# A fused attention, cosine layer and expert layer: the second token tile is summed in two parts, and four attention halves use another product form

## The chip, the cores and the metric

The kernel runs on one core of one Trainium2 chip. The metric is the device time of one execution in microseconds (us). Below, PE is the matrix engine (TensorE), DVE the vector engine (VectorE), ACT the scalar engine (ScalarE), POOL is GpSimd, and SP is the engine whose queue issues nearly all DMAs here. Every engine works through its own queue in order, and waits on semaphores for the others.

## The reference

Three steps follow each other, all in fp32.

```python
scores = scale * q @ k.T                      # 4 batches x 8 heads, 768 positions, 64 wide
keep   = (pos < n_sink) | (0 <= i - j < window)   # 4 first keys, and a window of 128
x  = softmax(where(keep, scores, -1e9)) @ v   # -> 3072 tokens x 512
h  = x @ w_in                                 # 512 -> 2048
y  = (h * cos(h)) @ w_out                     # 2048 -> 512
e  = argmax(y @ w_gate + bias[modality])      # one of 8 experts for each token
out = gate * relu(y @ w1[e]) @ w2[e]
```

The weights `w_in` and `w_out` come as 64-bit floats, and the kernel turns them into fp32 itself.

## The kernel before

Each fp32 product is made of three faster ones: an operand is split into a high part (`_h`, `_l` for the rest), and high by high, high by low and low by high are summed in PSUM. ACT copies the high part out of PSUM, DVE or POOL subtracts it to get the low part.

**Halves and tiles.** The 3072 tokens are 8 tiles of 384 (`NTILE`, numbers 0 to 7). Tile n is half a batch: even n the first 384 positions (three key blocks of 128), odd n the last 384 (four key blocks). The attention of one tile is called a half; it goes over 4 pairs of heads (`attn_front`, `mid`, `rest`). In `rest`, the normalised scores `Pb` are turned by PE (`pt`), split into `pT_h` and `pT_l`, the 16 columns of the first keys are copied out into `pc` and turned as well (`pz`, then `sp`), and the product with `v` is summed in `po`. From `STACK` on, a half uses the "stacked" form of the scores: both parts of a head lie over each other on 128 rows. The halves before it use 64 rows for each head, so two heads' products run beside each other.

**Blocks.** The cosine layer works on one tile and one slice `f` of 128 of the 2048 columns at a time; that is a block, 16 to a tile (`ffn_tile_gen`). A block makes `hp` (12 products of 384 columns on PE), DVE and ACT make `ch`, and ACT and POOL split it into `g_h` and `g_l`. Two blocks later its 9 products of 512 columns go into the three sums `y`. While the blocks of tile n - 1 run, the attention of tile n is woven in between: `run_ffn` emits as many blocks as a table of weights (`ATT_STEPS`, `STEPS_0`, `STEPS_1`) says. The list `seq` gives the order of blocks: 6 blocks of tile 0 (`F0`), 16 each of tiles 1 to 7, and the other 10 of tile 0 at the end. Between, the three partial sums of tile 0 lie in DRAM (`yp_scr`) and so do its inputs (`xs_scr`).

**Conversion.** `conv_gen` turns one slice of `w_in` and one of `w_out` for each of the 16 values of `f`: five DVE operations `cv_a` and one ACT operation for each of the 32 pieces, and the low part on POOL. `conv_to` paces it: 8 steps ahead, 4 steps a block in tile 0, and the rest over 16 blocks (`CSP`) of tile 1. A scheduler may move an instruction against its neighbours within the dependences.

**Routing.** When a tile's sum is complete, `route_tile` turns it (`yT`, 12 transposes), multiplies by the gate weights (`pl`, 12 products), picks the expert and stores the row. For the expert layer, tokens of one expert are gathered 256 at a time (a page, T = 0 to 13): `gather` computes the row numbers on DVE and issues two indirect DMAs on POOL into `m_yg`, `prelude` turns them (`m_a`), `first_product` and `second_product` follow, and the result is scattered to `out`. A page with 128 tokens or fewer takes the short form (`first_product_half`, `turn_half`). When the expert changes, `split` makes the new weights' high part on ACT and their low part on DVE for even and on POOL for odd pieces; `run(T)` gathers page T + 1 at its start.

Of the kernel before, what the change touches and what calls it, by code (L numbers as in the profile page):

```python
# [20 lines left out]
P = 128  # L21
# [15 lines left out]
STACK = 3  # L37
# [24 lines left out]
def kernel(  # L62
# [45 lines left out]
    xs_scr = [dram.tile([P, NPAIR * HALF], F32, name=f"xs_scr{i}") for i in range(2)]  # L108
    yp_scr = dram.tile([NQ, P, DM], F32, name="yp_scr")
# [129 lines left out]
    vp = apool.tile([P, 4, 5 * D], F32R, name="vp")  # L239
# [163 lines left out]
    def attn_front(hb, pr):  # L403
# [37 lines left out]
        kT_h = apool.tile([P, 4, SEG], F32R, name="kT_h")  # L441
# [6 lines left out]
        kT_l = kl[0]  # L448
# [20 lines left out]
        bs = [P, nblk - 1, NS]  # L469
        bj = [D, nblk - 1, NS]  # L470
        if stack:
            for j in range(2):
# [3 lines left out]
                if half == 0:  # L476
                    DVE.tensor_copy(ks_h[r, pr, :], kT[j][r, 0, 0:NS].bitcast(F32))
                    DVE.tensor_copy(ks_l[r, pr, :], kl[j][r, 0, 0:NS].bitcast(F32))
                DVE.tensor_copy(kT[j][r, 0:nblk - 1, P:SEG], ks_h[r, pr:pr + 1, :].to_broadcast(bj))
                DVE.tensor_copy(kl[j][r, 0:nblk - 1, P:SEG], ks_l[r, pr:pr + 1, :].to_broadcast(bj))  # L480
                kf = kT[j].rearrange("p t s -> p (t s)")[:, 0:nblk * SEG - NS].bitcast(F32)
                SP.dma_start(out=kf[hr[1 - j]], in_=kf[r])
        else:
            ACT.activation(out=kT_h[:, 0:nblk, 0:P], in_=pk3[:, 0:nblk, :], func=AF.Copy)
            tt(DVE, kT_l[:, 0:nblk, 0:P], pk3[:, 0:nblk, :], kT_h[:, 0:nblk, 0:P].bitcast(F32), ALU.subtract)
            if half == 0:
                DVE.tensor_copy(ks_h[:, pr, :], kT_h[:, 0, 0:NS].bitcast(F32))
                DVE.tensor_copy(ks_l[:, pr, :], kT_l[:, 0, 0:NS].bitcast(F32))
            DVE.tensor_copy(kT_h[:, 0:nblk - 1, P:SEG], ks_h[:, pr:pr + 1, :].to_broadcast(bs))
            DVE.tensor_copy(kT_l[:, 0:nblk - 1, P:SEG], ks_l[:, pr:pr + 1, :].to_broadcast(bs))  # L490
# [66 lines left out]
        def rest():  # L557
# [45 lines left out]
            xs = apool.tile([P, HALF], F32, name="xs")  # L603
# [9 lines left out]
            for j in range(2):  # L613
# [11 lines left out]
            ACT.activation(out=xh[:, pr, :], in_=xs, func=AF.Copy)  # L625
            tt(POOL, xl[:, pr, :], xs, xh[:, pr, :].bitcast(F32), ALU.subtract)
# [32 lines left out]
    def span(i):  # L659
        return (F0 if i == NTILE else 0), (F0 if i == 0 else NF)  # L660

    def start_of(i):
        return seq.index((i, span(i)[0]))

    def ffn_tile_gen(ypool_of):
        LAG = 2
# [23 lines left out]
        for c in range(n_all + LAG):  # L690
# [28 lines left out]
            if c == n_all + LAG - 3:  # L719
# [4 lines left out]
                ysb[NTILE] = [ypool_of().tile([P, YC], F32, name="yt", bufs=NQ) for _ in range(NQ)]  # L724
                for t in range(NQ):
                    SP.dma_start(out=ysb[NTILE][t][:, 0:DM], in_=yp_scr[t])
            i, f = seq[c - LAG] if c >= LAG else (0, -1)
            if f == span(i)[1] - 1:
                if i == 0:

                    for t in range(NQ):
                        yt = mpool.tile([P, DM], F32, name="y_part", tag="wo_l", bufs=WL_BUFS)
                        ACT.activation(out=yt, in_=yps[0][t], func=AF.Copy)
                        SP.dma_start(out=yp_scr[t], in_=yt)
                elif i == NTILE:
# [3 lines left out]
                    ysb[0] = ysb.pop(NTILE)  # L739
# [636 lines left out]
```

## Time and profile before

| what | value |
|---|---|
| median of three runs | 1231.5 us (1226.4 to 1232.37) |
| profiled execution | 1229.5 us, its span 1227.7 us |
| PE, DVE, ACT, POOL busy | 93%, 66%, 58%, 32% of the span |
| granted PE clock, mean | 0.963 of 2.4 GHz |

A busy PE is not a PE at its peak: a product counts as busy from its start to its modelled end, and products overlap. So the stretches with a slow clock and with gaps tell more than the mean. The stretch from 0 to 45 us is the first half's attention alone; blocks 0 to 5 run up to about 145 us, the 16 of tile 1 up to about 275 us, the 16 of tile 2 up to about 375 us, and the expert layer starts near 886 us.

### The profile page before, as it was taken

Reading aid. Unit: us, or ns where it says so; the run is one execution under the profiler, and the core shown is the slowest. Engines: PE = TensorE matmul, PEld = TensorE weight load, DVE = VectorE, ACT = ScalarE, POOL = GpSimd, SP = SyncE. Lnnn points to the kernel's source line nnn. Section 1 sums busy time; section 2 is a strip of 40 time slices with the busy share of each in tenths; the row PEclk is TensorE's granted clock in tenths of the full one; section 3 lists DMA queues with packets and bytes.
Section 4 is the critical chain, followed back from the end, with each engine's and each line's share of the span. In section 5 each row is a group of like instructions: output and inputs, shape, how many; then the busy total and the mean of one; then the engine's idle time right before and its main releaser. Section 6 shows DMA issues by size and latency. Waiting matters only on the chain. (4 is left out here: it accounts for less than half of the span.)

```text
span 1227.7 us, 21801 instructions
## 1 busy us (share of the span) xinstructions
PE 1143.7 (93%) x6560; PEld 1004.5 (82%) x6560; DVE 814.1 (66%) x2357; ACT 711.7 (58%) x1479; POOL 396.2 (32%) x422
## 2 busy tenths in 40 slices
PE   4878879889999999999999999999999999799995
PEld 3667767778988888988889888989889988699994
DVE  7788889987787788788878877464762224621220
ACT  4677667678876788777678876333422224522221
POOL 3655536552222322322232222142311113611110
PEclk9778888899999999999999999999999999899998
DMA  6444345533342333334324422361324113311210
GB/s 149 130 151 120 90 130 179 159 103 93 89 100 70 78 99 104 80 79 106 80 68 117 96 69 94 93 234 54 101 98 153 37 45 105 113 37 47 61 37 24
DMA packets 141338, 118.86 MB, mean 97 GB/s; under 512 B 98415, under 2 KB 107631, under 8 KB 141168
## 3 DMA queue, kind: packets, MB, share of 16 engines
q1 hardware_dynamic: 136848, 103.29, 30.5%
q0 software_dynamic: 4320, 13.65, 3.5%
q8 instruction: 65, 1.06, 0.4%
q14 instruction: 105, 0.86, 0.2%
HBM read 151.32 MB, written 19.67 MB: 139 GB/s over the span
## 5 line engine op out<-in xcount | busy, mean ns | idle before, releaser
L148 POOL TENSOR_TENSOR g_l<-ch,g_h 128x384 fp32r<-128x384 f32 x128 | 131.8, 1031 | 410.1 <-ACT g_h L715 393.7
L136 PE MATMUL hp<-xT_h,wi_h 128*128 128x384 f32 x512 | 184.7, 362 | 5.8 <-DVE ch L148 5.7
L136 PE MATMUL hp<-xT_h,wi_l 128*128 128x384 f32 x512 | 177.8, 347 | 0.0
L136 PE MATMUL hp<-xT_l,wi_h 128*128 128x384 f32 x512 | 177.6, 347 | 0.0
L643 PE MATMUL y<-wo,g_h 128*128 128x512 f32 x384 | 160.1, 417 | 0.0
L643 PE MATMUL y<-wo_l,g_h 128*128 128x512 f32 x384 | 157.9, 411 | 0.0
L643 PE MATMUL y<-wo,g_l 128*128 128x512 f32 x384 | 155.5, 405 | 0.2 <-POOL g_l L148 0.2
L136 PE MATMUL m_y<-wi_h,hT 128*128 128x512 f32 x416 | 134.1, 397 | 0.6 <-issue 0.4
L145 DVE SCALAR_TENSOR_TENSOR hT<-m_h,hT 128x256 fp32r<-128x256 f32 x88 | 37.3, 424 | 142.3 <-ACTq L1292 93.5
L705 ACT ACTIVATE ch<-ch,half_pi 128x384 f32<-128x384 f32 x128 | 78.8, 616 | 79.7 <-DVE ch L145 78.5
L136 PEld LDWEIGHTS hp<-xT_h,wi_h 128*128 128x128 f32 x512 | 99.3, 194 | 12.2 <-DVE ch L148 6.7
L136 PEld LDWEIGHTS hp<-xT_l,wi_h 128*128 128x128 f32 x512 | 99.3, 194 | 4.8 <-issue 0.7
L136 PEld LDWEIGHTS hp<-xT_h,wi_l 128*128 128x128 f32 x512 | 99.2, 194 | 0.7 <-issue 0.2
L142 DVE TENSOR_SCALAR ch<-hp 128x384 int32<-128x384 f32 x128 | 71.1, 555 | 41.8 <-PE hp L136 27.7
L715 ACT ACTIVATE g_h<-ch 128x384 fp32r<-128x384 f32 x128 | 66.5, 519 | 49.1 <-DVE ch L148 38.0
L136 PEld LDWEIGHTS m_y<-wi_h,hT 128*128 128x128 f32 x416 | 79.1, 190 | 17.1 <-issue 0.8
L1143 POOL DMA_INDIRECT out_dram<-m_ot,m_ids x26 | 26.3, 1011 | 204.9 <-ACT m_ot L1142 183.3
L554 ACT ACTIVATE Pb<-Pb,mx 128x272 f32<-128x272 f32 (+1 forms) x168 | 82.7, 493 | 11.5 <-DVE mx L538 10.4
L148 DVE TENSOR_TENSOR ch<-ch,hp 128x384 f32<-128x384 f32 x128 | 70.3, 550 | 24.8 <-ACT ch L705 23.2
L1111 ACT ACTIVATE hT<-m_h 128x256 fp32r<-128x256 f32 x88 | 33.7, 383 | 90.1 <-PE m_h L136 86.8
L643 PEld LDWEIGHTS y<-wo,g_l 128*128 128x128 f32 x384 | 73.2, 191 | 14.0 <-POOL g_l L148 0.7
L136 PE MATMUL m_y<-wi_l,hT 128*128 128x512 f32 x208 | 81.8, 393 | 0.0
(297 smaller groups left out, 3032.0 us busy)
## 6 DMA issues: line engine op xcount, KB each, us to landing
rw<-in_moe_w_dram SPq DMA_DIRECT2D x112, 512.0 KB
wo_l<-wl_scr SPq DMA_DIRECT2D x122, 256.0 KB
cv_in<-in_moe_w_in_dram SPq DMA_DIRECT2D x16, 512.0 KB
cv_out<-in_moe_w_out_dram SPq DMA_DIRECT2D x16, 512.0 KB
y_scr<-yt SPq DMA_DIRECT2D x24, 256.5 KB
xT_h<-xg_h SPq DMA_DIRECT2D x32, 192.0 KB
xT_l<-xg_l SPq DMA_DIRECT2D x32, 192.0 KB
qn<-in_q_dram SPq DMA_DIRECT2D x56, 96.0 KB
```

Source lines behind the costliest of these rows:

```text
L136: PE.matmul(o, l, r, start=start, stop=stop)
L142: e.tensor_scalar(out=o, in0=i, scalar1=s1, scalar2=s2, op0=op0, op1=op1)
L145: e.scalar_tensor_tensor(out=o, in0=i0, scalar=s, in1=i1, op0=op0, op1=op1)
L148: e.tensor_tensor(out=o, in0=a, in1=b, op=op)
L554: ACT.activation(out=Pb[t][j][:, c0:c1], in_=Pb[t][j][:, c0:c1], func=AF.Exp, scale=-1.0, bias=mx[:, i:i + 1], accum_out=sm[:, i:i + 1])
L643: i = PE.matmul(o, l, r, start=start, stop=stop)
L705: ACT.activation(out=ch, in_=ch, func=AF.Sin, scale=TWO_PI, bias=half_pi)
L715: ACT.activation(out=gh, in_=ch, func=AF.Copy)
L1111: ACT.activation(out=hT_h[f], in_=hp, func=AF.Relu)
L1143: POOL.indirect_dma_start(out=out[:, :], out_offset=bass.IndirectOffsetOnAxis(ap=m_ids[T % 4][:, h:h + 1], axis=0), in_=m_ot[h], in_offset ...
```

## The change

- **Order of blocks.** Tile 1 is summed in two parts as tile 0 is: its first 12 blocks (`F1`) stand where they stood, its last 4 come after tile 7 and ahead of tile 0's last 10. Its partial sums and inputs go through DRAM as well, and its routing comes at the end. Rows of `y_scr` are stored in the order of tiles 2 to 7, 1, 0.
- **Conversion.** `conv_to` spreads the steps after tile 0 over 12 blocks of tile 1 and 12 blocks of tile 2.
- **Halves 0 to 3** (`STACK` is 4) take another form of the product with `v`: both heads are summed in one `po`, with zeros beside each head's columns in `vp`. That is three products for each head and key block and not two, one copy on ACT and one subtraction on DVE for each pair; the two `xs` copies and two additions, and POOL's subtraction, are gone. Half 3 was stacked before and is not now.
- **POOL.** In halves 0 to 3 (`NPOOL` is 4) `pc` is copied on POOL and not on DVE; half 3's scaling of `Pb` goes to POOL too.
- **Small merges.** `ks_h` and `ks_l` become one tile, so two copies and two casts become one each.
- **Expert layer.** `split` uses DVE alone. The row numbers of page T + 2 are computed in page T, and its gather is issued ahead of page T's last scatter. The lead expert's weights are split in blocks near the end, some five later than before against the list.

```diff
-STACK = 3
+STACK = 4
-PB2 = 3
+PB2 = 4
+F1 = 12
-NPOOL = 3
+NPOOL = 4
-seq = [(i, f) for i in range(NTILE) for f in range(F0 if i == 0 else NF)] + [(NTILE, f) for f in range(F0, NF)]
+cut = {0: F0, 1: F1}
+late_of = {NTILE: 1, NTILE + 1: 0}
+seq = [(i, f) for i in range(NTILE + 2) for f in range(*span(i))]
...
-                        DVE.tensor_copy(pc[:, t, j], Pb[t][j][:, P:SEG])
+                        POOL.tensor_copy(pc[:, t, j], Pb[t][j][:, P:SEG])
...
+            if not stack:
+                po = psb("po")
+                mm(po[:, 0:HALF], vs[:, 0:2 * D], sp, True, False)
+                mm(po[:, 0:HALF], vs[:, 2 * D:4 * D], sp, False, False)
+                for j in range(2):
+                    for blk in range(nblk):
+                        c0, c1, m0, m1 = band(blk)
+                        vh, vl = [vp[:, blk, (o + j) * D:(o + j + 2) * D] for o in (0, 3)]
+                        mm(po[:, c0:c1], vh, pT_h[:, j, m0:m1], False, False)
+                        mm(po[:, c0:c1], vh, pT_l[:, j, m0:m1], False, False)
+                        mm(po[:, c0:c1], vl, pT_h[:, j, m0:m1], False, j == 1 and blk == nblk - 1)
+                ACT.activation(out=xh[:, pr, :], in_=po[:, 0:HALF], func=AF.Copy)
+                tt(DVE, xl[:, pr, :], po[:, 0:HALF], xh[:, pr, :].bitcast(F32), ALU.subtract)
...
-        tt(DVE if f % 2 == 0 else POOL, dst_l, src, dst_h.bitcast(F32), ALU.subtract)
+        tt(DVE, dst_l, src, dst_h.bitcast(F32), ALU.subtract)
...
-            with maybe(cond):
-                gather(T + 1, flags[T + 1, "col"])
+            with maybe(cond2):
+                gather_rows(T + 2, val(3, T + 2, (ET.DVE,), NV - 1))
+            def after():
+                with maybe(cond2):
+                    gather_go(T + 2)
...
-            second_product(T, 1, m_y[1])
+            second_product(T, 1, m_y[1], None, after)
```

Three places show how instructions moved.

PE, the product with `v` of one pair of heads in the third half, before: one head's products (the other head's seven follow, into another `po`).

```order
L136 MATMUL po<-sp,vs 128x384
L136 MATMUL po<-pT_h,vp 128x256
L136 MATMUL po<-pT_l,vp 128x256
L136 MATMUL po<-pT_h,vp 128x256
L136 MATMUL po<-pT_l,vp 128x256
L136 MATMUL po<-pT_h,vp 128x128
L136 MATMUL po<-pT_l,vp 128x128
```

The same place now: one head's part, after the two `sp` products that serve both heads.

```order
L137 MATMUL po<-sp,vs 128x384 x2
L137 MATMUL po<-pT_h,vp 128x256
L137 MATMUL po<-pT_l,vp 128x256
L137 MATMUL po<-pT_h,vp 128x256 x2
L137 MATMUL po<-pT_l,vp 128x256
L137 MATMUL po<-pT_h,vp 128x256
L137 MATMUL po<-pT_h,vp 128x128
L137 MATMUL po<-pT_l,vp 128x128
L137 MATMUL po<-pT_h,vp 128x128
```

Each key block has a third product, so a pair has 20 products and not 14 (26 and not 18 where there are four key blocks).

POOL, one pair of the third half beside tile 1, before (`wi_l`, `wo_l` are low parts of the conversion, `g_l` of a block).

```order
L142 TENSOR_SCALAR Pb<-Pb,sm 128x128 x2
L142 TENSOR_SCALAR Pb<-Pb,sm 128x272 x4
L148 TENSOR_TENSOR wi_l_2119<-cv_a,wi_h_2113 128x512
L148 TENSOR_TENSOR g_l<-ch,g_h 128x384
L148 TENSOR_TENSOR wo_l<-cv_a,wo_123 128x512
```

And now.

```order
L149 TENSOR_TENSOR wo_l<-cv_a,wo_121 128x512
L143 TENSOR_SCALAR Pb<-Pb,sm 128x128 x2
L143 TENSOR_SCALAR Pb<-Pb,sm 128x272 x2
L149 TENSOR_TENSOR g_l<-ch,g_h 128x384
L143 TENSOR_SCALAR Pb<-Pb,sm 128x272 x2
L601 COPY pc<-Pb 128x32
```

The copy `pc` stands on POOL right behind the pair's last scaling; on DVE it is gone.

POOL, end of one page of the expert layer (the long form's end is a scatter of half 0 and of half 1), before: the next page's two gathers come behind all of it, at the start of the next `run`.

```order
L148 TENSOR_TENSOR wi_l_95<-rw_9677,wi_h_85 128x512
L1292 UNCONDITIONAL_BRANCH x2
L1143 DMA out_dram<-m_ot_9707,m_ids_9696 3072x512
L1318 ISA
L1318 UNCONDITIONAL_BRANCH
L1255 TENSOR_LOAD tab_i x2
L1088 DMA m_yg_9681<-y_scr,m_idg_9694 128x513
L1088 DMA m_yg_9682<-y_scr,m_idg_9694 128x513
```

And now, the long form.

```order
L1191 DMA out_dram<-m_ot_10086,m_ids_10075 3072x512
L1134 DMA m_yg_10056<-y_scr,m_idg_10073 128x513
L1134 DMA m_yg_10057<-y_scr,m_idg_10073 128x513
L1191 DMA out_dram<-m_ot_10087,m_ids_10075 3072x512
L1374 UNCONDITIONAL_BRANCH
```

The gathers (of the page after the next) stand between the two scatters, and no `wi_l` is left on POOL.

## Rows read from the trace of the kernel before

**Rows 1.** The page: the span, and the granted PE clock in 40 slices.

```profile
span 1227.7 us, 21801 instructions
...
PEclk9778888899999999999999999999999999899998
```

**Rows 2.** Busy time by stretch; columns as the first line says.

```profile
core 0: us, PE busy (x) PEld busy (x) DVE busy (x) ACT busy (x) POOL busy (x), PEclk, DMA share, GB/s
0.00:45.00 45.00, 27.41 (x114) 20.72 (x114) 32.93 (x138) 23.57 (x66) 19.52 (x32) 0.97 0.56 137
45.00:145.00 100.00, 83.45 (x407) 67.67 (x407) 83.70 (x229) 70.27 (x169) 57.32 (x69) 0.77 0.42 121
145.00:275.00 130.00, 111.87 (x560) 91.40 (x559) 116.83 (x256) 92.92 (x192) 70.08 (x75) 0.91 0.50 146
275.00:375.00 100.00, 97.65 (x585) 87.27 (x584) 81.51 (x248) 79.06 (x155) 26.25 (x28) 1.00 0.38 92
1049.00:1056.00 7.00, 5.78 (x18) 4.78 (x18) 4.54 (x8) 5.11 (x12) 5.71 (x5) 0.52 0.85 278
```

**Rows 3.** DVE's groups by shape, 145 to 275 us: count, busy us, mean ns, idle before.

```profile
L145 DVE SCALAR_TENSOR_TENSOR cv_a<-cv_out,cv_a 128x512 int32<-128x512 int32 x19 | 19.4, 1022 | 0.1
L142 DVE TENSOR_SCALAR ch<-hp 128x384 int32<-128x384 f32 x17 | 9.4, 551 | 4.1 <-PE hp L136 4.0
L148 DVE TENSOR_TENSOR xs<-po,xs 64x384 f32<-64x384 f32 x10 | 5.5, 555 | 0.6 <-ACT xs L623 0.3
L592 DVE COPY pc<-Pb 128x32 f32<-128x32 f32 x4 | 2.8, 709 | 1.3 <-POOL Pb L142 1.3
L487 DVE COPY ks_h<-kT_h 128x16 f32<-128x16 f32 x4 | 2.6, 648 | 0.0
```

**Rows 4.** The same, DVE, 45 to 145 us.

```profile
L590 DVE COPY pc<-pb_x 128x16 f32<-128x16 f32 x14 | 5.4, 420 | 0.3 <-POOL pb_x L142 0.3
L592 DVE COPY pc<-Pb 128x96 f32<-128x96 f32 x2 | 2.0, 1022 | 0.0
```

**Rows 5.** The same, DVE, 0 to 45 us.

```profile
L487 DVE COPY ks_h<-kT_h 128x16 f32<-128x16 f32 x3 | 0.5, 166 | 0.0
L590 DVE COPY pc<-pb_x 128x16 f32<-128x16 f32 x2 | 0.3, 162 | 0.0
```

**Rows 6.** POOL's groups by shape, 145 to 275 us.

```profile
L148 POOL TENSOR_TENSOR wi_l<-cv_a,wi_h 128x512 fp32r<-128x512 f32 x8 | 10.5, 1309 | 14.5 <-ACT wi_h L305 13.5 <-PE pt L579 1.0
L142 POOL TENSOR_SCALAR Pb<-Pb,sm 128x272 f32<-128x272 f32 x16 | 9.9, 631 | 0.2 <-DVE ks_l L488 0.2
L142 POOL TENSOR_SCALAR Pb<-Pb,sm 128x128 f32<-128x128 f32 x8 | 3.6, 458 | 4.0 <-DVE sm L561 3.5 <-DVE sm L140 0.5
```

**Rows 7.** Products of `hp` alone in two stretches of plain blocks near the end.

```profile
826.20:842.90 16.70, 9.06 (x48) 8.53 (x48) 6.67 (x12) 1.00 0.22 64
843.00:867.90 24.90, 12.17 (x61) 10.33 (x61) 7.82 (x15) 1.00 0.19 54
```

**Rows 8.** Timeline around 1047 us: start, us, instruction, idle before and what ended it.

```profile
1044.17 0.66 PE L1127 MATMUL m_t<-ident,h_sb 128*128 128x128 f32 x4
1046.09 0.26 ACT L1130 ACTIVATE hT<-m_y 128x128 fp32r<-128x128 f32 x1
1047.62 4.93 POOL L148 TENSOR_TENSOR wi_l<-rw,wi_h 128x512 fp32r<-128x512 f32 x4
1048.79 0.33 PE L1100 MATMUL m_a<-ident,m_yg 128*128 128x128 f32 x1 [3.96 <-DMA m_yg<-y_scr,m_idg]
1051.75 0.77 PE L136 MATMUL m_y<-wi_h,hT 128*128 128x512 f32 x1
1056.11 0.39 PE L136 MATMUL m_y<-wi_l,hT 128*128 128x512 f32 x1
1059.10 0.39 PE L136 MATMUL m_y<-wi_h,hT 128*128 128x512 f32 x1
```

More of the change, by code (lines that the diff above doesn't have):

```diff
@@ L44 @@
 F0 = 6
+F1 = 12
+LAG_T = 2
 CSP = 16
@@ L107 @@
     wl_scr = dram.tile([NF, P, DM], F32, name="wl_scr")
-    xs_scr = [dram.tile([P, NPAIR * HALF], F32, name=f"xs_scr{i}") for i in range(2)]
-    yp_scr = dram.tile([NQ, P, DM], F32, name="yp_scr")
+    xs_scr = [[dram.tile([P, NPAIR * HALF], F32, name=f"xs_scr{n}{i}") for i in range(2)] for n in range(2)]
+    yp_scr = [dram.tile([NQ, P, DM], F32, name=f"yp_scr{n}") for n in range(2)]
     y_scr = dram.tile([NT, YC], F32, name="y_scr")
@@ L486, in attn_front @@
             if half == 0:
[L487 to L490, printed above, removed]
+                DVE.tensor_copy(ks[:, pr], kT2[:, :, 0, 0:NS].bitcast(F32))
+            DVE.tensor_copy(kT2[:, :, 0:nblk - 1, P:SEG], ks[:, pr].unsqueeze(2).to_broadcast(bs))
         yield steps(hb)[0]
@@ L718, in ffn_tile_gen @@
                 load_wo(c)
-            if c == n_all + LAG - 3:
+            if c in ends:
                 for r_ in routes:
@@ L1020 @@
             run_ffn(min(tgt, t1_ - 0.01))
-    run_ffn(start_of(NTILE - 1) + 2.5)
-    attn_x(NTILE)
-    for i_ in range(2):
-        SP.dma_start(out=xT[NTILE][i_].rearrange("p c x -> p (c x)").bitcast(F32), in_=xs_scr[i_])
+    for n_ in late_of:
+        run_ffn(start_of(n_ - 1) + 2.5)
+        attn_x(n_)
+        for i_ in range(2):
+            SP.dma_start(out=xT[n_][i_].rearrange("p c x -> p (c x)").bitcast(F32), in_=xs_scr[late_of[n_]][i_])
     late_st.close()
@@ L1036 @@
     m_it = [fin.tile([P, 2], F32, name=f"m_it{i}") for i in range(4)]
+    m_ix2 = [fin.tile([P, 2], F32, name=f"m_ix2{i}") for i in range(4)]
     m_idg = [fin.tile([P, 2], U32, name=f"m_idg{i}") for i in range(4)]
@@ L1076, in gather, with gather_rows @@
     def gather(T, col, rows=NT):
+        gather_rows(T, col)
+        gather_go(T, rows)
+    def gather_rows(T, col):
         i = T % 4
@@ L1131, in turn_half, with second_product @@
             tt(DVE, hT_l[f][:, 0:P], pt[:, s], hT_h[f][:, 0:P].bitcast(F32), ALU.subtract)
-    def second_product(T, h, yp, between=None):
+    def second_product(T, h, yp, between=None, behind=None):
         i = T % 2
@@ L1142, in second_product @@
         ACT.activation(out=m_ot[h], in_=yp, func=AF.Copy, scale=m_yg[i][h][:, DM:YC])
+        if behind is not None:
+            behind()
         POOL.indirect_dma_start(out=out[:, :], out_offset=bass.IndirectOffsetOnAxis(ap=m_ids[T % 4][:, h:h + 1], axis=0),
@@ L1281 @@
         second_product(0, 0, m_y[0])
-        second_product(0, 1, m_y[1], lambda f: prelude(1, m_a) if f == PPF else None)
+        gather_rows(2, val(3, 2, (ET.DVE,), NV - 1))
+        second_product(0, 1, m_y[1], lambda f: prelude(1, m_a) if f == PPF else None, lambda: gather_go(2))
     m_h = [ps_h(f"m_h{i}") for i in range(2)]
@@ L1302, in run, with ahead @@
             load_flags(T + 1)
-            with maybe(cond):
-                gather(T + 1, flags[T + 1, "col"])
-        def ahead():
+        after = None
+        if T + 2 < NSUP:
+            cond2 = flags.get((T + 2, "valid"))
+            cond2 = cond2 > 0 if cond2 is not None else None
+            with maybe(cond2):
[3 more added lines that the diff above has]
+                    gather_go(T + 2)
+        def ahead(behind=None):
             if T > 1:
@@ L1311, in ahead @@
                     prelude(T + 1, m_a)
-            second_product(T, 0, m_y[0], (lambda f: on_change(T + 1, f, split_w1)) if more else None)
+            second_product(T, 0, m_y[0], (lambda f: on_change(T + 1, f, split_w1)) if more else None, behind)
         def split_ahead(f):
@@ L1330, in run @@
                 turn_half(g, m_t[g])
-            ahead()
+            ahead(after)
         if more and cond is not None:
```

101 lines of the change are left out of this document (60 added, 41 removed).

## The prediction

> **What bounds the kernel now.** I read the page's span and its row of granted clocks first, then busy time by stretch, then the groups of the busiest engine by shape, and last the timeline of one gap. The clock is low only in the first fifth, and once near the end [rows 1]. The stretches [rows 2] show two regimes. From 275 us on PE is the bound: 97.65 of 100 us busy at clock 1.00, DVE 81.51. In the first 275 us PE is busy for 27.41 + 83.45 + 111.87 = 222.7 us, 81%, and DVE for 32.93 + 83.70 + 116.83 = 233.5 us, or 73%, 84% and 90% of the three stretches, though the clock was 0.97, 0.77 and 0.91. With two levels (1.2 and 2.4 GHz), 0.77 means that some 46 of 100 us were granted the lower one, 0.91 some 23 of 130 us. PE waits there for others, and each of the three counts. I take DVE for the bound of the first 275 us, and value work taken from it at its share of the stretch: 1 us less of DVE work is worth 0.73, 0.84 or 0.90 us.
>
> The second regime is plain: four blocks without attention take 16.70 us, 4.2 us each, and the same with a tile's end and routing 24.90 us [rows 7].
>
> **DVE's work in the first 275 us.** The copies `pc` leave DVE: two at 0.162, 0.3 us [rows 5]; 5.4 + 2.0 = 7.4 us [rows 4]; 2.8 us [rows 3]. Of the two additions `xs` for each pair one subtraction is left, so each of twelve pairs saves one of 0.555 us [rows 3]: 0.6, 6 x 0.555 = 3.3, and 5 x 0.555 = 2.8 us. The merged `ks` saves one copy and one cast for each pair: six of 0.166 [rows 5] are 1.0 us, four of them 0.7 us, and in the last stretch about the 2.6 us of the four copies [rows 3], with a little more 3.0 us. Of the conversion the order moves only nine of 128 DVE operations behind tile 2's first block, whatever the new pace says: 9 x 1.022 = 9.2 us [rows 3]. And four of tile 1's blocks leave, each with three operations on `ch` of 0.551 us: 6.6 us [rows 3].
>
> The sums are 0.3 + 0.6 + 1.0 = 1.9 us, 7.4 + 3.3 + 0.7 = 11.4 us and 2.8 + 2.8 + 3.0 + 9.2 + 6.6 = 24.4 us. At the shares above they are worth 1.4 + 9.6 + 22.0 = **33.0 us**.
>
> **PE's added work.** A pair of halves 0 and 2 gets 1,280 more columns of `po`, a pair of halves 1 and 3 gets 1,536 (count of the products, less the second `sp` pair). Four plain blocks have 48 products of 384 and 36 of 512 columns, 36,864 in 16.70 us [rows 7]: 0.453 ns a column. That is 2.3 us for an even half, 2.8 us for an odd one, 7.4 us for halves 0 to 2, and 8.5 us at the clocks of rows 2 weighted by place. It fills gaps where DVE is the bound, and costs all where PE is. I charge the middle, 4.3 us, with 0 and 8.5 as bounds. Net for the first 275 us: 4.3 - 33.0 = **-28.7 us**.
>
> The copies and scalings that POOL takes over: half 3's scaling is 24 operations of at most 0.631 us [rows 6], 15.1 us, in a stretch where POOL was busy for 26.25 of 100 us [rows 2], so I cost it at nothing; uncovered it would be all 15.1. A `pc` copy on POOL isn't in the trace. The nearest row is its smallest scaling, 0.458 us [rows 6], and the dearest that it can stand behind is a low part of 1.309 us. In the forecast half 0 to 2's POOL share (0.43, 0.57, 0.54) [rows 2] hides it; the price if it doesn't is rival A.
>
> **Beside tile 2 (275 to 375 us).** PE is the bound. Tile 1's routing leaves: 24.90 us is five blocks (5 x 4.18 = 20.9) and 4.0 us of tile's end [rows 7]. Half 3's product with `v` adds 2.8 us. Net **-1.2 us**.
>
> **At the end** all that left comes back at plain price, in a regime where PE is at 1.00 and nothing hides it: four blocks 16.7 us, the end of a tile 4.0 us [rows 7]. The stores and loads of the partial sums go through SP, which has 44 blocks' time and more for them (nothing). The lead weights' split starts some ten blocks later; I charge 0.5 us, between 0 and 2 (two low parts late at 1.309 us rounded down). Sum **+21.2 us**.
>
> **The expert layer.** One gap is in reach. PE turned page 6's tokens until 1044.83 us (1044.17 + 0.66), then waited 3.96 us for the gather `m_yg` of page 7, and its next product `m_y` began at 1051.75, behind POOL's four `wi_l` of 4.93 us in all [rows 8]. The change takes both: the gather is issued a page earlier, and no low part is left on POOL. What remains is `hT`, from 1046.09, and the low parts on DVE alone. If these last no longer than they did on two engines together, `m_y` starts near 1047.7 us, 4.0 us sooner. The stretch from 1049 to 1056 us ran at 0.52 [rows 2], close to the lower level throughout; without the idle time ahead of it half of 7 x 0.48 = 3.4 us comes back, 1.7. Together **-5.5 us** (rounded down; from -3 with the low parts late to -8 with all of the gap). Elsewhere in the expert layer I expect nothing: the later products of the same weights follow at once [rows 8].
>
> **Sum.** -28.7 - 1.2 + 21.2 - 5.5 = -14.2 us. The profiled execution took 1229.5 us, 2.0 below the median of 1231.5, so 1215.3 becomes **1217 us**.
>
> **A rule that speaks against it.** DVE's copies cost more the more POOL and the conversion do beside them: a `ks_h` copy took 0.166 us in the first 45 us [rows 5] and 0.648 us in the third stretch [rows 3]; `pc` 0.162 [rows 5] against 0.420 [rows 4] for the same shape. So most of a `pc` copy may be a wait for POOL, and POOL's copy may keep DVE out in turn. If it does, the sum is rival D's.
>
> The Trainium skill (SBUF — State Buffer, "SBUF: two separate sides") has a rule for this: one pair of ports serves both engines, an instruction of GpSimd holds it to its end, and a VectorE instruction that needs it (a copy in its fast mode, or one with two inputs in SBUF) waits in full. By that rule moving a copy to POOL only turns the lock round, and the time would be that of rival D. The rows agree in direction; which engine waited in them they don't show.
>
> **Rivals.**
>
> A, slower: *POOL's order.* PE's `pz`, `sp` and the rest of `po` now wait for a copy that stands in POOL's queue behind low parts of 1.309 us [rows 6]. If PE meets one such low part and the copy (1.31 + 0.46 = 1.8 us) or the low part alone (1.3 us) at each of 16 pairs, that is 21 to 29 us; with the pairs of half 1 that have several copies up to 33. From -14.2 this gives 1238 to 1250, say **1244**. It decides from 0.9 us a pair on (14.2 / 16), and is slower by over half a per cent from 1.3 us. For it: POOL's scaling waited 3.5 of its 4.0 us for DVE [rows 6], so the chain of one pair already runs through both queues. Against it: POOL idles for 43% and more of each stretch [rows 2], and blocks' products lie between.
>
> B, little changed: *PE's order and clock set the first 275 us*, and DVE's 90% is a consequence. Then only the four blocks leave, at the clock of that stretch 16.7 / 0.91 = 18.4 us, and the new products cost their 8.5: -9.9 and not -28.7. The sum is -9.9 - 1.2 + 21.2 - 5.5 = +4.6, **1236**. For it: the low clock of 0.77 in the stretch where DVE was busy for only 84%. Against: in the third stretch DVE idled for 13.2 us and PE for 18.1 [rows 2], and the one longer wait among DVE's groups there is 4.0 us for `hp` [rows 3].
>
> C, faster still: *the clock recovers.* 46 + 23 = 69 us ran at the lower level and cost up to half, 34 us. If denser PE work in halves 0 to 2 gives a third of that back, 11 us, the time is **1206**.
>
> D, *DVE gains less than it loses work*: copies on POOL keep DVE out for as long as its own copies took, which takes back 0.3 + 7.4 + 2.8 = 10.5 us at 0.85, 9 us: **1226**. For it: the same copy's 0.162 and 0.420 us [rows 4, 5]. That the change doesn't do what it says ends here too: if the nine conversion operations find no room behind tile 1 either, 9.2 x 0.90 = 8.3 us are lost, 1225.
>
> **How the numbers follow.** The forecast has a chance of 0.50, A 0.12, B 0.16, C 0.12, D 0.10. The forecast's own range is 1207 to 1226, from PE's cost (4.3 either way), the gap (2.5) and the lead weights (1.5), added up. Half a per cent, 6 us, is about what a measurement of this kernel can tell from no change: faster is below 1225.3, slower above 1237.7. Faster: 0.48 of the forecast, C, half of D: 0.65. Slower: 0.09 of A, 0.04 of B: 0.13. The rest is 0.22. The range of 8 in 10 goes from 1202 (C with 15 us back) to 1238 (B, and the low end of A); outside lie most of A and the far end of C.
>
> **What would show it.** In the profile after: the first block of tile 2 should begin near 275 - 28.7 = 246 us, the expert layer near 886 - 8.7 = 877 us. DVE's busy time up to there should be some 30 us lower, and its share still above PE's in the third stretch; if DVE's share falls while the stretch is as long, B holds. A shows as PE's idle time ahead of `pz` and `po` put down to `pc` on POOL, and as `pc` rows of a microsecond and more. D shows as means of DVE's remaining copies and additions that rise. C shows as a clock above 0.77 in blocks 0 to 5. The four late blocks should take 4.2 us each and one more tile's end 4 us. On page 6 the wait for `m_yg` should be gone, with `m_y` waiting for the low parts alone. The forecast falls with its largest term: if DVE is not what PE waits for in tile 1, 22 us of the gain aren't there.

## The result and the profile after

The changed kernel takes 1247.33 us (median of four, 1242.89 to 1250.6), the kernel before 1231.93 us (median of four): 1.013 of it, with a 95% interval of 1.0087 to 1.0173. It is slower, where the prediction said faster, and lies outside the range. The profiled execution's span is 1244.8 us, 17.1 more than before.

The page of the changed kernel, span and granted clock in 40 slices, beside [rows 1]:

```profile
span 1244.8 us, 21882 instructions
...
PEclk9889899989999999999999999999999999999998
```

The clock is higher than before in the first slices, yet the time is longer. The stretches tell where (busy time by stretch, same columns as [rows 2]); the bounds are the first `hp` of tile 2 (249.9), of tile 3 (359.6), of the four late blocks (822.4), of the last block (890.9), and the first long page's `m_h` (934.4):

```profile
core 0: us, PE busy (x) PEld busy (x) DVE busy (x) ACT busy (x) POOL busy (x), PEclk, DMA share, GB/s
0.00:45.00 45.00, 25.73 (x114) 19.39 (x114) 33.19 (x125) 20.92 (x58) 19.16 (x34) 0.99 0.55 134
45.00:145.00 100.00, 82.43 (x464) 68.54 (x462) 79.46 (x211) 68.10 (x161) 56.37 (x82) 0.85 0.44 128
145.00:249.90 104.90, 91.85 (x505) 74.60 (x504) 82.39 (x197) 74.45 (x155) 53.09 (x65) 0.93 0.55 162
249.90:359.60 109.70, 104.12 (x599) 89.58 (x598) 70.30 (x179) 75.34 (x147) 44.34 (x62) 0.95 0.32 88
822.40:890.90 68.50, 64.64 (x343) 57.87 (x342) 44.13 (x116) 27.55 (x48) 15.44 (x15) 0.98 0.49 163
890.90:934.40 43.50, 40.53 (x254) 35.20 (x253) 31.20 (x149) 9.89 (x20) 5.61 (x6) 1.00 0.24 80
934.40:1244.80 310.40, 287.46 (x1793) 257.28 (x1791) 90.67 (x252) 86.85 (x190) 50.03 (x49) 0.98 0.21 70
```

The same marks in the kernel before are 275.2, 374.9, 838.8, 880.6 and 919.7 us. So:

| stretch | before | after | difference | predicted |
|---|---|---|---|---|
| up to tile 2's first block (after: four blocks fewer) | 275.2 | 249.9 | -25.3 | -28.7 |
| tile 2's blocks | 99.7 | 109.7 | +10.0 | -1.2 |
| tiles 3 to 7 | 463.9 | 462.8 | -1.1 | 0 |
| late blocks, to the last one (before: 9 steps; after: 13) | 41.8 | 68.5 | +26.7 | +21.2, with the next row |
| last block to the first long page | 39.1 | 43.5 | +4.4 | |
| from there to the end | 308.0 | 310.4 | +2.4 | -5.5 |

The forecast's sum was -14.2 us, that of the profiled executions is +17.1. Of these 31.3 us, 3.4 lie ahead of tile 2, 11.2 beside it, 9.9 at the end and 7.9 in the expert layer, less 1.1 in tiles 3 to 7.

**The first 250 us.** POOL's group of the moved copy, 45 to 250 us (instructions by line and shape), beside [rows 4]:

```profile
L599 POOL COPY pc<-pb_x 128x16 f32<-128x16 f32 x14 | 2.7, 228 | 0.0
```

It took 0.228 us where DVE took 0.420. But DVE now stands still. What DVE waited for, 45 to 250 us (engine, what it did next and for whom it waited; total, times, longest):

```profile
DVE cv_a L143 <- POOL wo_l L149: 10.2, 5, 3.3
DVE cv_a L143 <- POOL wi_l L149: 6.6, 5, 2.7
```

In the kernel before, 45 to 275 us, the same wait was:

```profile
DVE cv_a L142 <- POOL wi_l L148: 1.5, 2, 1.0
```

**Tile 2.** PE's waits in 249.9 to 359.6 us, and behind them those of the kernel before in 275.2 to 374.9 us:

```profile
PE ps L137 <- DVE mx L547: 3.9, 2, 2.1
PE ps L137 <- DVE xT_l L149: 0.9, 1, 0.9
```

```profile
PE ps L136 <- DVE mx L538: 0.8, 1, 0.8
PE pt L578 <- DVE ks_h L477: 0.7, 1, 0.7
```

**The late blocks.** DVE's timeline of the changed kernel around 862 us:

```profile
861.37 1.29 DVE L149 TENSOR_TENSOR wi_l<-rw,wi_h 128x512 fp32r<-128x512 f32 x2 [1.79 <-ACT wi_h L1097]
863.18 0.55 DVE L149 TENSOR_TENSOR ch<-ch,hp 128x384 f32<-128x384 f32 x1 [0.51 <-ACT ch L735]
```

ACT's wait from 858 to 864 us (total, times, longest):

```profile
ACT wi_h L1097 <- DMA rw<-in_moe_w_dram: 2.5, 3, 1.8
```

PE's timeline around 862 and 909 us:

```profile
863.79 0.69 PE L137 MATMUL hp<-xT_h,wi_h 128*128 128x384 f32 x1 [2.28 <-DVE ch L149]
909.01 0.66 PE L791 MATMUL yT<-ident,yt 128*128 128x128 f32 x4 [1.93 <-DVE yt L149]
```

ACT waits for the lead expert's weights (`rw`), their low part therefore waits at the head of DVE's queue, a block's `ch` stands behind it, and PE waits 2.28 us. Later PE waits 1.93 us for tile 0's sum. SP's timeline shows why, first of the kernel before, then of the changed one:

```profile
872.87 0.32 SPq L726 DMA_DIRECT2D yt<-yp_scr  x1
```

```profile
900.91 2.90 SPq L832 DMA_DIRECT2D y_scr<-yt  x3
905.56 1.61 SPq L757 DMA_DIRECT2D yt<-yp_scr  x3
```

Before, tile 0's partial sums were asked for 16 us ahead of their use (889.0 us); now at 905.56 us, because the three buffers `yt` still held tile 1's rows, whose stores were issued from 900.91 us on.

**The expert layer.** PE's timeline on pages 6 and 7, beside [rows 8]:

```profile
1057.57 0.39 PE L137 MATMUL m_h<-wi_h,m_xT_l 128*128 128x512 f32 x1 [2.54 <-issue]
1064.21 1.04 PE L1146 MATMUL m_a<-ident,m_yg 128*128 128x128 f32 x8
1079.45 0.50 PE L137 MATMUL m_h<-m_x,wi_h 128*128 128x256 f32 x2 [2.55 <-DVE hT L146]
```

The wait for `m_yg` is gone (`m_a` runs at 1064.21 without one), and `m_y` follows at once. But PE stands 2.54 us in page 6's first product, for nothing that the profile shows, and 2.55 us in page 7's. The second wait isn't new; in the kernel before it was

```profile
1068.50 0.51 PE L136 MATMUL m_h<-m_x,wi_h 128*128 128x256 f32 x2 [1.82 <-DVE hT L145]
```

What DVE did before that `hT` in the changed kernel:

```profile
1073.52 3.69 DVE L149 TENSOR_TENSOR wi_l<-rw,wi_h 128x512 fp32r<-128x512 f32 x6
1078.97 0.42 DVE L146 SCALAR_TENSOR_TENSOR hT<-m_h,hT 128x256 fp32r<-128x256 f32 x1
```

Between the two lines lie the row numbers of a later page, from 1077.49 to 1079.02 us. Both the low parts on DVE alone and the row numbers at this place are the change's. From page 6's first product to page 8's it was 1036.9 to 1086.2, 49.3 us; it is 1052.4 to 1100.2, 47.8 us. The other 3.9 us of the row's +2.4 were lost elsewhere: 1.0 on page 1, 0.7 on pages 8 to 12, 2.4 from page 13 to the end, less 0.2 on pages 2 to 5.

### The profile page after: what moved, and what is told of

Its sections match the earlier page's. It is cut to its first block, busy times and chain, and to the rows that moved or that the text cites. A ratio compares the mean times of both kernels' runs of the same rounds, so it can differ in the third digit from the quotient of the medians.

```text
span 1244.8 us, 21882 instructions
## 1 busy us (share of the span) xinstructions
PE 1150.8 (92%) x6696; PEld 1007.8 (81%) x6696; DVE 786.0 (63%) x2304; ACT 690.3 (55%) x1427; POOL 364.6 (29%) x436
## 5 line engine op out<-in xcount | busy, mean ns | idle before, releaser
L735 ACT ACTIVATE ch<-ch,cols 128x384 f32<-128x384 f32 x128 | 78.8, 616 | 105.2 <-DVE ch L146 102.3
L137 PEld LDWEIGHTS hp<-xT_h,wi_h 128*128 128x128 f32 x512 | 99.0, 194 | 11.9 <-DVE ch L149 4.4
L149 DVE TENSOR_TENSOR ch<-ch,hp 128x384 f32<-128x384 f32 x128 | 70.3, 550 | 31.0 <-ACT ch L735 29.3
L137 PE MATMUL ps<-kT_hl,qT_h 64*128 64x272 f32 (+3 forms) x288 | 60.6, 351 | 31.1 <-DVE xT_l L149 11.2
```

Source lines behind the costliest of these rows:

```text
L137: PE.matmul(o, l, r, start=start, stop=stop)
L149: e.tensor_tensor(out=o, in0=a, in1=b, op=op)
L735: ACT.activation(out=ch, in_=ch, func=AF.Sin, scale=TWO_PI, bias=half_pi)
```

## The experiments

Ratios are to the kernel before on the same chip, with 95% intervals. "C" is the changed kernel.

**1. C without the cut of tile 1** (the conversion's pace, the gather's row formula and the lead weights' place in the list are as before too, and aren't shown):

```diff
-cut = {0: F0, 1: F1}
-late_of = {NTILE: 1, NTILE + 1: 0}
+cut = {0: F0}
+late_of = {NTILE: 0}
```

> The changed kernel with tile 1 summed in one part again: 16 blocks after tile 0's six, its routing beside tile 2, the conversion's pace and the lead weights' times as in the kernel before. All else of the change stays. Theory 1 (the cut costs more than it frees: the late part of the trace grew by 26.7 us from block 118 to the last block, and 4.4 us more passed from there to the first long page, because the lead expert's weights now come behind tile 7's routing): these 31 us leave, tile 2 gets routing back (3 us) and loses conversion (2 us), and the first 250 us get four blocks and nine conversion operations, 14 to 18 us: 1228 to 1234 us. Theory 2 (the terms of the prediction were right about the cut and other parts of the change lost the time): the cut is worth 14.2 + 4.0 in front and 21.2 behind, so the time falls by 3 us only, 1244 us. Theory 3 (the cut is what made the first 275 us faster): above 1250 us.

1226.87 us, 0.9971 (0.9948 to 0.9993). Theory 1, and a little more: the cut with what belongs to it costs some 20 us, and what is left of the change gains 3.5. Its stretches:

```profile
45.00:144.60 99.60, 81.44 (x457) 67.91 (x456) 78.68 (x210) 67.64 (x159) 54.55 (x82) 0.85 0.45 128
144.60:270.40 125.80, 108.16 (x594) 90.95 (x592) 102.98 (x227) 84.17 (x172) 67.18 (x74) 0.92 0.50 146
270.40:375.40 105.00, 103.27 (x638) 90.21 (x636) 66.50 (x199) 71.80 (x140) 36.60 (x56) 1.00 0.28 74
```

Uncut, tile 2 begins at 270.4 us, only 4.8 sooner than before, and takes 105.0 us, 5.3 longer, so that tile 3 begins at 375.4 us where it began at 374.9: in this trace the front gains nothing, and where the 3.5 us of the medians come from isn't shown. The cut brings tile 2 forward to 249.9, by 20.5 us, and then loses 4.7 us in tile 2; behind, late blocks take 41.8 us uncut, and 39.1 us pass to the first long page, as before.

**2. C with half 3 as before:**

```diff
-STACK = 4
-PB2 = 4
-NPOOL = 4
+STACK = 3
+PB2 = 3
+NPOOL = 3
```

> The changed kernel with half 3 as before (stacked form, its scaling and its copies where they were); only halves 0 to 2 have the new form. Theory 1 (the unstacked half 3 costs PE beside tile 2: 3.6 us of po, 2.0 us of ps that the prediction left out, and its waits for mx with the slow clock behind them): the stretch of tile 2's blocks falls from 109.7 to 100 to 103 us, the time to 1238 to 1241 us. Theory 2 (the waits of 3.9 us and the slow clock of 10.2 us there come from the conversion that now runs into tile 2): only the products go, 5.6 us, the waits for DVE stay, 1241 to 1243 us. Theory 3 (DVE's work matters there, of which half 3 stacked has more): 1247 us or more.

1253.45 us, 1.0198 (1.0154 to 1.0241). Tile 2's blocks take 94.0 us, less than theory 1 said, but tile 1's twelve take 124.0 and not 105.8. In that stretch (144.1 to 268.1 us) stands a wait that C has not:

```profile
PE pz L604 <- DVE pT_l L149: 6.1, 1, 6.1
```

Of the 18.2 us that tile 1's twelve blocks lost, 11.9 are idle time of PE (25.0 us of 124.0, for 13.1 of 105.8) and 6.3 longer products, at a granted clock of 0.85 for 0.94. The time fits theory 3, its reason only in part: all 128 DVE operations of the conversion now ran ahead of tile 2, where C left 14 of them, 11.6 us, to tile 2. So this run moved the conversion too, and doesn't tell the price of half 3's form by itself.

**3 and 4. C with the low parts of the expert weights on DVE and POOL in turn; C with each page's gather where it was:**

```diff
-tt(DVE, dst_l, src, dst_h.bitcast(F32), ALU.subtract)
+tt(DVE if f % 2 == 0 else POOL, dst_l, src, dst_h.bitcast(F32), ALU.subtract)
```

> The changed kernel with the odd pieces' low parts of the expert weights on POOL again, in every page. Theory 1 (DVE's queue holds blocks' ch and the routing behind low parts that wait for the weights: 2.28 us of PE idle at block 122 and a slow clock behind it): the late part falls by 3 to 5 us, and page 6 pays up to 4 us for POOL's slow low parts: 1243 to 1248 us. Theory 2 (the weights themselves come late, whoever splits them): the late part moves by 1 us or less, page 6 gets slower, 1247 to 1251 us.

```diff
-gather_rows(T + 2, ...)          # and gather_go(T + 2) ahead of the last scatter
+gather(T + 1, val(3, T + 1, (ET.DVE,), NV - 1))
```

> The changed kernel with each page's gather at the start of the page before, as in the kernel before, and not two pages ahead and before the last scatter. Theory 1 (the early gather saves what the prediction said, 4 us on page 6, and something else made the expert layer longer): 1250 to 1253 us, PE waits for m_yg on page 6 again. Theory 2 (the early gather and the longer branch code cost as much as they save: PE stands for 2.54 us in the middle of page 6's first product, for 2.55 us in page 7's and 0.94 us in the last one's, each time for nothing that the profile shows): these gaps of 6 us go, the wait of 4 us comes back, 1244 to 1248 us.

Run 3: 1247.29 us, 1.0135 (1.0092 to 1.0179). PE's gap near block 122 is 4.0 us and not 2.28: the weights come late, whoever splits them (theory 2). Run 4: 1241.52 us, 1.0100 (1.0071 to 1.0129), below both theories. The wait for the gather is back:

```profile
1061.12 0.47 PE L1146 MATMUL m_a<-ident,m_yg 128*128 128x128 f32 x1 [4.55 <-DMA m_yg<-y_scr,m_idg]
```

and yet page 6's first product to page 8's takes 46.8 us (1047.8 to 1094.6), 1.0 less than with the early gather. For the whole kernel neither a saving nor a cost of the early gather is shown: the intervals of run 4 and C overlap, and the uncut kernel with the late gather is level with the early one:

> Tile 1 in one part, and each page's gather as in the kernel before; all else as changed. Theory 1 (the gather's new place costs 3 to 6 us, as between the changed kernel and the one with the late gather, in pages that stand for nothing that the profile shows): 1221 to 1224 us. Theory 2 (that difference was of executions; in the trace of the uncut kernel the expert layer takes 308.4 us with the early gather, 308.0 us before): 1226 to 1229 us.

1226.30 us, 0.9973 (0.9955 to 0.9991), theory 2. Page by page (from its first product to the next page's) the traces say more:

| traces | page 6, us | page 7, us | first long page to the end, us |
|---|---|---|---|
| expert layer as before (before, 9, 13 and the two other orders: 7) | 20.5 to 22.8 | 24.8 to 29.0 | 305.5 to 311.8, mean 309.5 |
| as in C (C, 1, 2, 5, 6, 8, 10, 11, 12, 14: 10) | 15.9 to 21.0 | 27.9 to 29.3 | 305.1 to 312.2, mean 308.8 |
| late gather (4, 7: 2) | 23.3 and 21.7 | 23.5 and 23.5 | 307.1 and 305.5 |

The early gather does save 3 to 4 us on page 6, nearly as predicted, and page 7 pays 4 to 5 for it, of which C's trace shows 2.55 as the wait for `hT`. And traces of one and the same expert layer differ by 6 to 7 us, so the +2.4 of the table above can't be told from nothing.

**5 and 8. Three buffers for `cv_a`**, in C and in the uncut kernel:

```diff
-a = cpool.tile([P, 512], I32, name="cv_a", bufs=2)
+a = cpool.tile([P, 512], I32, name="cv_a", bufs=3)
```

> The changed kernel with three buffers for cv_a and not two: the conversion's first operation on DVE no longer stands for the low part that POOL makes of the operation but one before. Theory 1 (DVE does less in the first 250 us but stands idle at cv_a for POOL's wi_l and wo_l, 16.8 us from 45 to 250 us, with xT_l and mx behind it, for which PE waits 7.9 and 6.8 us in one piece near 133 us): these idle times fall below 5 us, tile 2's first block starts at 238 to 243 us and not at 249.9, the time is 1236 to 1241 us. Theory 2 (the waits only mark where PE's own chain of products, softmax and turns is late; DVE would wait for something else there): the idle time goes to other operations, 1245 to 1249 us.

> Tile 1 in one part, and three buffers for cv_a; all else as changed. Theory 1 (DVE's idle time at cv_a is on the path): the 16 blocks of tile 1 end at 258 to 264 us and not at 270.4, 1216 to 1221 us. Theory 2 (it is not): 1225 to 1229 us.

1246.69 us, 1.0149 (1.0113 to 1.0184), and 1230.11 us, 1.0008 (0.9985 to 1.0030): no gain (the second is above theory 2's range). In run 5, 45 to 255 us, DVE still waits at `cv_a`:

```profile
DVE cv_a L143 <- POOL wi_l L149: 7.0, 5, 2.1
...
DVE cv_a L143 <- POOL wo_l L149: 6.5, 4, 2.2
```

With another buffer the conversion ran further ahead (73 of its DVE operations ahead of tile 1's first block, for 63 in C) and then stood at the same place. Tile 1's first block began 11.2 us later, and tile 1's and tile 2's blocks then took 5.4 and 6.9 us less; in run 8 it was 7.4 us later and tile 1 took 7.4 less. The loss moved and didn't go. My first theory for the front, that these waits are its price, falls.

**6, 9 and 14. Where `pc` is copied**, in C, in the kernel before (there halves 0 to 2 on POOL) and in the uncut kernel. One of the two lines of runs 6 and 14; run 9's is the reverse:

```diff
-(POOL if hb < NPOOL else DVE).tensor_copy(pc[:, t0:], Pt[:, t0:, :, P:SEG])
+DVE.tensor_copy(pc[:, t0:], Pt[:, t0:, :, P:SEG])
```

> The changed kernel with the copies pc of halves 0 to 3 on DVE again. Theory 1 (the prediction's: DVE's work counts at its share of the stretch): 10.5 us come back on DVE in the first 250 us, 8 to 9 us of time: 1255 to 1257 us. Theory 2 (DVE stands for POOL's low parts in this stretch, so what is put on POOL holds DVE as well; a pc copy took POOL 0.228 us and DVE 0.42 to 0.7): between -2 and +3 us, 1245 to 1250 us.

> The kernel before with one change: the copies pc of halves 0 to 2 on POOL. Theory 1 (the copies are what the change gained in front, 9 us by the prediction and 7 us between the changed kernel and the one with pc on DVE, and the new product form with its one po gained nothing or lost): 1220 to 1225 us. Theory 2 (the copies pay only beside the new form, whose pairs wait longer for DVE): 1228 to 1232 us. Theory 3 (PE waits for pc behind POOL's low parts): above 1236 us.

> Tile 1 in one part and the copies pc on DVE, all else as changed: the new product form without the move of the copies. With the kernel before (neither), the kernel with the copies alone moved (5.4 to 6 us slower) and the uncut kernel (both, 3.5 us faster) this makes a table of two by two. Theory 1 (the two changes help each other only together): 1231 to 1236 us, as the changed kernel lost 7.4 us when the copies went back to DVE. Theory 2 (the new form alone carries the gain and the copies' place is worth nothing): 1225 to 1228 us.

1254.73 us, 1.0204 (1.0163 to 1.0244); 1236.53 us, 1.0044 (1.0017 to 1.0071); 1239.88 us, 1.0068 (1.0036 to 1.0101). Run 6 came out next to theory 1, the prediction's, and missed theory 2; run 9 has theory 3's time; run 14 lies above both theories. So the copies' move alone costs 5 us, all else of the uncut change (the new form, the merges, half 3, the expert layer) 8 us, and both together save 3.5 us. A fixed price per operation can't do that; an order of queues can. In run 9 PE waits for DVE's `xs`, not for `pc` (its waits, 45 to 282.3 us):

```profile
PE ps L136 <- DVE xs L148: 11.5, 9, 2.8
PE pt L578 <- DVE xs L148: 5.8, 2, 4.9
```

In the kernel before, 45 to 275.2 us, these two were 6.7 and 2.7 us.

**10 and 12. C with the lead expert chosen from tiles 2 to 6; and also tiles of their own for tile 0's sums:**

```diff
-gather(0, e0 * NTI, NT - 2 * HALF)
+gather(0, e0 * NTI, NT - 3 * HALF)   # lead() ahead of the last late tile's load
```

> The changed kernel with the lead expert chosen from tiles 2 to 6 and not 2 to 7, so that its weights are asked for some 13 blocks earlier, as in the kernel before; the splits' places in the list stay. Theory 1 (the 10 us that the late part and the way to the first long page took above plain price come from weights that arrive late and low parts that hold DVE's queue): from block 114 to the last block 62 to 64 us and not 68.5, 40 us and not 43.5 from there to the first long page, 1237 to 1241 us. Theory 2 (they come from two routings and two loads of partial sums close together, whatever the weights do): 1245 to 1248 us.

```diff
+yl += [fin.tile([P, YC], F32, name=f"y_l{t}") for t in range(NQ)]
+if yl and c == n_all - 7:
+    SP.dma_start(out=yl[t][:, 0:DM], in_=yp_scr[0][t])   # for each t
...
```

> As the kernel with the early lead expert, and tile 0's partial sums are loaded seven blocks before the end into tiles of their own, not into the three that tile 1's routing frees last. Theory 1 (after the last block 4 to 5 us were lost because the load of tile 0's sums was issued at 902 us, behind tile 1's rows, and PE waited 2.56 us for it at yT; in the kernel before it was issued at 873 us): from the last block to the first long page 39 to 41 us and not 44.1, 1238 to 1241 us. Theory 2 (PE has other work there anyway and the two routings themselves are the price): 43 to 44 us, 1242 to 1245 us.

1243.70 us, 1.0098 (1.0072 to 1.0124), between the two theories, and 1239.59 us, 1.0072 (1.0047 to 1.0098), theory 1. In run 10 the late blocks take 64.1 us and not 68.5, at a clock of 1.00 where C had 0.98:

```profile
822.50:886.60 64.10, 62.69 (x343) 56.39 (x342) 39.14 (x95) 24.54 (x41) 13.22 (x13) 1.00 0.34 100
```

The way to the first long page stays at 44.1 us, with PE's wait at `yT`:

```profile
905.31 0.66 PE L791 MATMUL yT<-ident,yt 128*128 128x128 f32 x4 [2.56 <-DVE yt L149]
```

In run 12 that wait is gone and the way takes 42.1 us. Each of the two delays is thus shown by its removal, in the stretches; the intervals of the whole times overlap from one run to the next. 3 us of the way (42.1 against 39.1) remain, and I haven't found them.

**11. C with the conversion paced over tile 1 as before:**

```diff
-elif at < F0 + F1 + NF:   # two slopes, over F1 blocks of tile 1 and of tile 2
+elif at < F0 + NF:
+    conv_to(CONV_LEAD + 4 * F0 + int(4.0 * (NF - F0) * min(1.0, (at - F0) / CSP)))
```

> The changed kernel with the conversion paced over tile 1 as in the kernel before (the 12 blocks that are left of it take all but the last steps). Theory 1 (conversion that runs into tile 2 holds DVE in front of mx, for which PE waited 3.9 us at a tile that PE bounds, with 10.2 us of slow clock): tile 2's blocks take 101 to 104 us and not 109.7, tile 1's 3 to 5 us more, 1242 to 1245 us. Theory 2 (the conversion costs the same wherever it lies): 1246 to 1250 us.

1247.51 us, 1.0139 (1.0076 to 1.0201). Tile 2 takes 105.2 us, 4.5 less, tile 1's part 109.0, 3.2 more: what was moved (6 of the 14 late operations) costs about the same in either place (theory 2).

**13, and two other orders. Is DVE's work the price of the first 275 us?** The kernel before without one of the conversion's four DVE operations for each piece (the trace has 128 for 32 pieces, so four and not five as said above), then two other orders of the kernel before, each with and without that operation:

```diff
-stt(DVE, a, s, TINY_SQ, a, ALU.is_ge, ALU.mult)
```

> The kernel before without the conversion's operation on DVE that sets tiny numbers to zero (128 x 512, one for each of 32 pieces, 0.72 us each; this part of the computation is left out). Nothing in the attention depends on it. From 45 to 250 us that is 28 operations, 20.2 us of DVE's busy time. Theory 1 (the prediction's: DVE is what the first 275 us wait for, 1 us of its work is worth 0.84 to 0.90 us): 17 us less, 1212 to 1215 us. Theory 2 (the first 275 us are a chain of PE, DVE, ACT and POOL for each pair of heads, in which DVE's share is high but the order of its queue decides; relief shifts the waits): at most 6 us less, 1224 to 1232 us.

```diff
-S_FIRST = 1.082
-ATT_STEPS = (1.092, 0.997)
+S_FIRST = 1.06
+ATT_STEPS = (1.07, 1.01)
```

> The kernel before with other weights in the table that spreads the attention over the blocks (S_FIRST 1.06 for 1.082, ATT_STEPS 1.07 and 1.01 for 1.092 and 0.997): the same instructions in another order. Theory 1 (the work on DVE sets the first 275 us): the order is worth 2 us or less. Theory 2 (the order of the queues sets it): 4 us or more either way, and the run with less DVE work at this order need not follow.

> The order of j1 and, beside it, the conversion's operation that sets tiny numbers to zero left out (part of the computation). Theory 1 (DVE's work has a price of its own): 15 to 17 us below j1. Theory 2 (the order decides): between 0 and 6 us below j1.

```diff
-STEPS_0 = (1.57,1.25,3.7,1.39,1.89,5.32,1.04,1.73)
-STEPS_1 = (1.57,1.25,4.13,2.21,1.93,4.62,1.04,1.52)
+STEPS_0 = (1.57,1.25,3.9,1.39,1.89,5.1,1.04,1.73)
+STEPS_1 = (1.57,1.25,4.3,2.21,1.93,4.4,1.04,1.52)
```

> The kernel before with other weights of the single steps of a pair (STEPS_0 and STEPS_1: third 3.9 and 4.3 for 3.7 and 4.13, sixth 5.1 and 4.4 for 5.32 and 4.62): the same instructions, a third order. Theory 1: within 2 us of the kernel before. Theory 2: 4 us or more either way.

> The order of j2 without the conversion's operation that sets tiny numbers to zero (part of the computation is left out). Theory 1 (DVE's work has a price of its own): 15 to 17 us below j2. Theory 2 (the order decides): between 0 and 6 us below j2.

| order | all work, us | less DVE work, us | tile 2's first block |
|---|---|---|---|
| before | 1230.22 (ratio 1) | 1229.56, 0.9983 (0.9952 to 1.0013) | 275.2, then 271.6 |
| first other | 1238.52 (1229.21 before, here and below), 1.0058 (1.0008 to 1.0109) | 1234.81, 1.0033 (0.9986 to 1.0080) | 280.7, then 275.1 |
| second other | 1241.11, 1.0098 (1.0048 to 1.0147) | 1225.86, 0.9964 (0.9914 to 1.0015) | 285.5, then 270.8 |

Run 13's stretches, to be read against [rows 2]:

```profile
45.00:145.00 100.00, 82.31 (x424) 68.96 (x425) 82.00 (x225) 73.84 (x177) 53.95 (x70) 0.79 0.46 129
145.00:271.60 126.60, 107.17 (x546) 87.65 (x545) 99.50 (x230) 90.10 (x184) 69.28 (x75) 0.91 0.49 146
```

DVE's share of the third stretch fell from 90% to 79%. Tile 2 began 3.6 us sooner, and the kernel's time fell by nothing that can be told. PE still waited for DVE, for other results (run 13, 45 to 271.6 us):

```profile
PE pt L577 <- DVE qT_l L148: 6.2, 3, 2.9
PE pt L577 <- DVE xs L148: 5.9, 3, 4.5
PE ps L136 <- DVE xs L148: 5.9, 7, 2.4
```

In the other orders the same work was worth 3.7 us, which the intervals don't tell from nothing, and 15.3 us, which is theory 1's figure and a miss for the theory that I argue. So DVE's work has no fixed price: some 20 us of it were worth 3.6, 5.6 and 14.7 us by tile 2's first block in three orders, and the order alone moved the kernel by 7 to 12 us by the ratios, with the same computing instructions (these two orders have three runs each).

What these gains consist of is a surprise. From 45 us to tile 2's first block PE's busy time fell by 6.0, 6.0 and 14.0 us (195.5 to 189.5, 196.2 to 190.2, 202.6 to 188.6, with as many products); its idle time changed by +2.4, +0.4 and -0.7. The granted clock moved little (0.85 and 0.85, 0.88 and 0.90, 0.84 and 0.86). So by the profile, in which the ends of products are modelled, the relief shortened PE's products and not its waits. Why it did isn't shown.

## Why the prediction was wrong

**The step that failed first: "I take DVE for the bound of the first 275 us, and value work taken from it at its share of the stretch."** This made 33.0 us. Run 13 takes 20.2 us of DVE's work away, for which that step asks 17: the kernel gains under 1 us (6 at most by the interval), and tile 2 begins 3.6 us sooner. A share of 90% says that an engine is rarely idle; what PE waited for was single results of DVE, and with less work it waited for others as long. Each pair of heads goes PE, DVE, POOL, PE, ACT, DVE. That the order of the queues matters is shown by the two other orders; at which link is not. The uncut kernel shows it for the change itself: the terms for `pc`, `xs`, `ks` and the new product's cost come to 18.7 - 4.3 = 14.4 us by the prediction's steps, and tile 2 began 4.8 us sooner, of which nothing was left at tile 3.

**That the first row of the table came out near (-25.3 for -28.7) was an accident.** The four blocks and the conversion, priced at 14.2 us, gave 20.5 (rival B had the blocks at 18.4), and of that 4.7 were lost again in tile 2. Not nine operations of the conversion went behind tile 2's first block but 14, 11.6 us.

**Beside tile 2** (-1.2, measured +10.0). The prediction counted half 3's `po` but not its `ps`: by the distance from start to start less idle time, `ps` went from 6.5 to 8.5 us (48 and 70 products) and `po` from 8.4 to 12.0, where 2.8 was charged. Routing gave 3.1 back, not 4.0. PE's idle time grew by 3.3 us, most of it waits for `mx` (0.8 to 3.9 us), and the blocks' own products took 4.0 us longer at the slower clock (0.95 for 1.00). Part of both comes with the conversion that now lies there: run 11, which moved some of it back, took 4.5 us off this stretch.

**The end** (+21.2, measured 26.7 + 4.4 = 31.1). Blocks and routing were priced nearly right: 20.7 us, and with the lead weights early (run 10) the late blocks take 22.3 more than before. What failed is "nothing" for the loads of partial sums and "0.5 us" for the lead weights. Run 10 takes back 4.4 us of the late blocks; run 12 shows that the late load into occupied buffers (at 905.56 us in C) was another 2.

**The expert layer** (-5.5, measured +2.4). Both waits named did go, and page 6 got shorter by 2.6 us in C and by 3 to 4 through the early gather (runs 4 and 7). What the prediction left out is the price on page 7: DVE now makes all low parts and the row numbers, and PE waits behind them for `hT`. What the 2.54 us of page 6 wait for isn't in the trace. On the average of the traces the layer gained 0.7 us, far less than their spread.

**The rivals.** The time lies in A's range of 1238 to 1250 us, which is luck, since A's mechanism isn't there: PE never waits for `pc` in the list of waits, and `pc` took 0.228 us. B's premise (DVE's share is a consequence) is the one that run 13 supports, but its sum is off too: -9.9 us ahead of tile 2, measured -25.3. C's clock did recover (0.77 to 0.85 from 45 to 145 us, and the same in the uncut kernel), and tile 1 began no sooner: by the uncut kernel's trace, less idle time, PE's other products took 4.9 us less, the new `po` 3.2 more, and PE idled 1.6 longer. For D, the Trainium skill (SBUF — State Buffer, "SBUF: two separate sides") has VectorE and GpSimd lock one pair of ports against each other, and by that the prediction would have the copies' move give nothing. Here it cost 5 us alone and saved 7 to 13 us beside the new form (runs 6, 9 and 14). D's sign shows in one small group: the merged `ks` copy took DVE 0.220 us with `pc` on DVE (run 14) and 0.408 with `pc` on POOL (run 1), 0.9 us over five; the subtractions `xT_l` kept their 0.549. So no run here isolates the ports. That the conversion's pace matters little was right in sum (run 11).

## What to carry to other kernels

Before pricing work taken from a busy engine, ask which of its results the next engine waits for; where several in-order queues feed each other, test the price by leaving some of the work out, in more than one order. Differences under some 10 us in such a stretch can be the order's and no part's, so an edit that reorders queues needs the comparison at a second order. Work moved to the end of a pipeline is paid there at full price, and with it all that counted on the old end: which data is complete when the next stage picks its first weights, and which buffers its last loads take.

## What the hardware showed that I had not expected

- The same computing instructions in another order: 1238.5 and 1241.1 us for 1229.2.
- Some 20 us less of DVE's work shortened PE's products by 6 to 14 us in all and changed its idle time by +2.4 to -0.7.
- Two parts of a change that each make the kernel slower (1.0044 and 1.0068) make it slightly faster together (0.9971).
- A granted clock of 0.85 for 0.77 over 100 us of attention, and tile 1's first block no sooner (99.6 us and 99.8 us from 45 us on): 51 more products and more idle time took what it gave.
- POOL copied 128 x 16 numbers in 0.228 us where DVE, beside the conversion, took 0.420.
